# Twenty-four one-pass float32r products ahead of one FFN1 block of a gated-attention and multiplicative-FFN kernel

## The chip, the cores and the metric

The kernel runs on one core of one Trainium2 chip. The core has five engines that run their own instruction streams: PE (TensorE, matrix products), DVE (VectorE), ACT (ScalarE), POOL (GpSimd) and SP (SyncE, which here only starts transfers). They meet at semaphores. The metric is the device time of one execution in microseconds (us); the time of a kernel is the median of its runs.

## The reference, cut to what matters

```python
# attention: 4 batches, 8 heads, 768 positions, head size 48
for t in range(S):
    S_re, S_im = ar * S_re - ai * S_im + kv, ar * S_im + ai * S_re   # kv = outer(k_t, v_t), a clipped to magnitude 0.999
    y[:, :, t] = einsum('bhd,bhde->bhe', q[:, :, t], S_re)
# bridge: x is 3072 tokens x 384
# FFN, d_ff = 1024
a = x @ w1
b = x @ w2
h = a * b @ w3          # (a * b) @ w3
out = h @ w_out
```

Everything is float32. (Some lines are contracted here.)

## The kernel before, in words

The 3072 tokens are cut into eight **units** u = 0 to 7; a unit is half of one batch, 384 positions (TT), and has three chunks of 128. For a unit the kernel does:

- the **gates** (`gates`, elementwise work on tiles of 128x1152 on ACT and DVE): logarithms, exponentials, running products and angles turn the complex recurrence into scaled q and k; 12 transfers of SP then move them to the layout that PE reads (tiles `KL`, `QL`);
- the **attention** on PE: transposes (`turn`, L766, tile `tp`, copied out by ACT at L768), the state (`state`, L830, `kv`), scores inside a chunk (`scores`, L780, `sc`, masked by DVE at L783 into `A`), outputs (`outputs`, L813, `y`), which ACT copies to `xT` (L815), 128 x 3 x 384: the unit's tokens, transposed, with the 384 channels in three rows of 128;
- **FFN1** (`ffn_ab`): for each of eight blocks j of 128 hidden channels two halves. The first half is three products of 128x128 (weights `w1s`) by 128x384 (`xT`) into a PSUM tile `m` (L852), copied by ACT to `a` (L857). The second is the same with `w2s`, and DVE multiplies its PSUM tile with `a` into `ab` (L859);
- **FFN2** with `w3 @ w_out`, multiplied out once at the start (`fuse`, L1150). Two tiles of tokens at a time are done with seven smaller products in place of eight (`out_pair`, L912, tile `p`), on sums that DVE forms (`out_sums`, L887, `So`); DVE and ACT add the products up, SP writes the result out.

PE's program is one list that `pieces`, `ffn` and `unit` put together: the attention of unit u+1 is laid between the FFN of unit u. So FFN1 of unit 3 stands in the list of unit 4: eight halves (blocks 0 to 3) at its head, then the rest between unit 4's transposes and states. The gate work on ACT and DVE is laid beside this list by a planner with an estimated clock per engine (`run`, `fill`, `TIMES`); whatever it decides, each engine then executes its instructions strictly in the order in which they were written down. The planner counts time per list item by `TIMES`, not by the instructions that an item's function issues.

Two rings of buffers matter for the change. PSUM tiles `m` come from `ps_m`, four buffers in turn; a buffer is written again when the one who read it four allocations ago is done. The tiles `a` come from `two` with the tag "a", two buffers in turn.

POOL runs a check over the weights and gates through the whole middle of the program (L1036 to L1072, tiles `look` and `seen`); nobody waits for it until the end.

Of the kernel before, what the change touches and what calls it, by code (L numbers as in the profile page):

```python
# [9 lines left out]

FP = mybir.dt.float32
I32 = mybir.dt.int32
U32 = mybir.dt.uint32
U16 = mybir.dt.uint16
# [10 lines left out]
def general(ctx, tc, qt, kt, v, art, ait, w1, w2, w3t, wo, w1s, w2s, w3o, ident, out):  # L25
# [42 lines left out]

    Qb = [singles.tile([P, 3, S], FP, name=f"Q{i}") for i in range(2)]
    Kb = [singles.tile([P, 2, S], FP, name=f"K{i}") for i in range(2)]  # L70
    Xb = [singles.tile([P, 3, S], FP, name=f"X{i}") for i in range(2)]
    Ab = [singles.tile([P, 2, NC, C], FP, name=f"A{i}") for i in range(2)]
    Db = [singles.tile([P, 2, NC, SB], FP, name=f"D{i}") for i in range(2)]

    sl = singles.tile([P, SB], I32, name="sl")
    nc.gpsimd.iota(sl, pattern=[[0, SB]], base=0, channel_multiplier=1)
    nc.vector.tensor_scalar(out=sl, in0=sl, scalar1=SB - 1, scalar2=None, op0=OP.bitwise_and)
    diag = singles.tile([P, SB], I32, name="diag")  # L80
    nc.gpsimd.iota(diag, pattern=[[1, SB]], base=0, channel_multiplier=0)
    nc.vector.tensor_tensor(out=diag, in0=sl, in1=diag, op=OP.is_equal)
    masks = {}
    for i, n in enumerate((1, 2, 4, 8, 16)):
        m = singles.tile([P, SB // 2], I32, name=f"mask{n}")
        half = singles.tile([P, SB // 2], I32, name=f"half{n}")
        nc.gpsimd.iota(m, pattern=[[2, SB // 2 // n], [0, n]], base=0, channel_multiplier=0)
# [7 lines left out]
    def load_unit(u):  # L95
# [6 lines left out]
        e0 = 2 * hp * D  # L102
        v_t[u] = two.tile([P, NC, 2 * D], FP, tag="v", name="v")
        nc.sync.dma_start(out=v_t[u], in_=v[b, :, e0:e0 + 2 * D].rearrange("(c p) e -> p c e", p=C))
# [197 lines left out]
    def weights(dst, src):  # L302
        if src.dtype == FP:
            return [lambda: nc.sync.dma_start(out=dst, in_=src)]
        r, m = dst.shape[1:]
        src = src.bitcast(I32)
        step = min(r, max(1, LOAD // m)), min(m, LOAD)
# [4 lines left out]
    def convert(dst, src):  # L312
        r, m = dst.shape[1:]
        raw = two.tile([P, r, m, 2], I32, tag="raw", name="raw")
        nc.sync.dma_start(out=raw.rearrange("p r m w -> p r (m w)"), in_=src)
# [61 lines left out]
def kernel(  # L377
# [36 lines left out]
    nc = tc.nc  # L414
    B, H, D, S = qt.shape
    P = 128
# [4 lines left out]
    KD = DM // P  # L421
    DG = P // H
    KF = FF // P
    WB = 2 * P
    HEAD = 16
    VLOAD = 3
    SIGN_DVE = (1,)
    SPLIT = (0,)
    TT = S // 2
# [28 lines left out]
    two = fast.enter_context(tc.tile_pool(name="two", bufs=2))  # L458
    ps_s = fast.enter_context(tc.tile_pool(name="ps_s", bufs=1, space=PSUM))
    ps_v = fast.enter_context(tc.tile_pool(name="ps_v", bufs=2, space=PSUM))  # L460
    ps_m = fast.enter_context(tc.tile_pool(name="ps_m", bufs=4, space=PSUM))
# [33 lines left out]
    g_t, L_t, xT_t, ab_t, T_t, KT_t = {}, {}, {}, {}, {}, {}  # L495
# [49 lines left out]
    def load_v(u):  # L545
        b, h = divmod(u, 2)


        vr = one.tile([P, UC, DM], FP, tag="vr", name="vr")
        nc.sync.dma_start(out=vr, in_=v[b, h * TT:(h + 1) * TT].rearrange("(c p) e -> p c e", p=C))  # L550
        g_t[u]["vr"] = vr
# [292 lines left out]
    def ffn_ab(u, j):  # L844
        got = []

        def half(w):
            if j == 0 and not got:
                ab_t[u] = one.tile([P, KF, TT], FP, tag="ab", name="ab")
            m = ps_m.tile([P, TT], FP, tag="mm", name="m")  # L850
            for f in range(KD):
                nc.tensor.matmul(out=m, lhsT=w[:, j * P // WB, f, j * P % WB:j * P % WB + P], rhs=xT_t[u][:, f],  # L852
                                 start=(f == 0), stop=(f == KD - 1))
            with tc.high_priority():
                if not got:
                    got.append(two.tile([P, TT], FP, tag="a", name="a"))
                    nc.scalar.copy(out=got[0], in_=m)  # L857
                else:
                    last["ab", u, j] = nc.vector.tensor_tensor(out=ab_t[u][:, j], in0=m, in1=got[0], op=OP.mult)  # L859
        return [("ab1", lambda: half(w1s)), ("ab2", lambda: half(w2s))]  # L860
# [7 lines left out]
    def out_weights():  # L868
        T = s_t["T"] = late[0].tile([P, 4, KH, DH], FP, tag="T", name="To")
        B = [[w3o[:, i * KH:(i + 1) * KH, j * DH:(j + 1) * DH] for j in range(2)] for i in range(2)]  # L870
        s_t["B"] = B[0][0], B[1][0], B[1][1], T[:, 3], T[:, 0], T[:, 1], T[:, 2]
        for i, x, y in ((0, B[0][1], B[0][0]), (1, B[1][1], T[:, 0]), (2, B[1][1], B[0][1]), (3, B[1][0], T[:, 1])):
            yield "DVE", 0.96, "out", ()
            nc.vector.tensor_tensor(out=T[:, i], in0=x, in1=y, op=OP.subtract)
# [212 lines left out]
    got = {}  # L1087
# [36 lines left out]
    def row_load(f, parts=1):  # L1124

        step = FF // parts
        w3_t[f] = fetch([columns(w3t, 0, step)[:, f:f + 1], words(wo)[:, f:f + 1]] +
                        [columns(w3t, n * step, (n + 1) * step)[:, f:f + 1] for n in range(1, parts)],
                        {0: "KL", 1: "QL"}.get(f % 4))
# [58 lines left out]
    def pieces(u):  # L1188

        sc = [[("sc", lambda c=c, x=x: scores(u, c, x)) for x in range(2)] for c in range(UC)]  # L1190
        tr = [[("tr", lambda c=c, x=x: turn(u, c, x)) for x in range(2)] for c in range(UC)]
        kv = [("kv0" if u % 2 == c == 0 else "kv" if c < UC - 1 else "rho", lambda c=c: state(u, c)) for c in range(UC)]
        y = [("y" if u % 2 or c else "y0", lambda c=c: outputs(u, c)) for c in range(UC)]

        if u % 2:
            return [[("need", u), tr[0][0]], [tr[0][1]], [tr[1][0], kv[0]], [tr[1][1]], [kv[1]], sc[0], sc[1] + [y[0]],
                    sc[2] + [y[1], y[2], ("end", u)]]
        return [[("need", u), tr[0][0]], [tr[0][1]], [tr[1][0], kv[0]], [tr[1][1]], [tr[2][0], kv[1]], [tr[2][1]],
                [kv[2]] + sc[0], sc[1] + [y[0]], sc[2] + [y[1], y[2], ("end", u)]]
# [19 lines left out]
    def mixed(items, fills, at):  # L1219

        seq = []
        for n, x in enumerate(items + [None]):
            seq += [fills[i] for i, k in enumerate(at) if k == n] + [x]
        return seq[:-1]

    def unit(u, rest, ahead):

        if u == 1:
            return [("begin", u)] + mixed([x for p in pieces(u) for x in p], rest, FILLS[1])
        seq = [("begin", u)] + rest[:ahead]  # L1230
        rest = rest[ahead:]
        p = pieces(u) + [[]]
        n = len(p)
        first = [i * (len(rest) - 2) // (n - 1) for i in range(n)] + [len(rest)]
        for i in range(n):
            seq += rest[first[i]:first[i + 1]] + p[i]
        return seq
# [43 lines left out]
    def run(seq):  # L1281
# [78 lines left out]

        heads = [k for k, (kind, f) in enumerate(seq) if kind == "ab1"][:HEAD // 2:2]
        for o in urgent:
# [50 lines left out]
    with tc.manual_schedule(engines={mybir.EngineType.PE}):  # L1413
# [9 lines left out]
        for f in range(KF):  # L1423
# [3 lines left out]
            if f + 4 < KF:  # L1427
                row_load(f + 4)
            if f == VLOAD:
                load_v(0)  # L1430
# [13 lines left out]
        with tc.manual_schedule(engines={mybir.EngineType.Activation, mybir.EngineType.DVE, mybir.EngineType.Pool, mybir.EngineType.SP}):  # L1444
# [12 lines left out]
            def head(i):  # L1457
                if i % 4 == 0:
                    force(i // 4)
                rest[i][1]()  # L1460
                if i == HEAD - 4:
                    phase.close()
                    late.append(fast.enter_context(tc.tile_pool(name="late", bufs=1)))
                    late.append(fast.enter_context(tc.tile_pool(name="looks", bufs=1)))
                    looks.append(check_weights(late[1]))
                    streams.append((1, out_weights()))
            seq = mixed([x for p in pieces(0) for x in p], fills, FILLS[0]) + [("begin", 0)] + [(rest[i][0], lambda i=i: head(i)) for i in range(HEAD)]
            for u in range(1, NU):
                seq += unit(u, rest[HEAD:] if u == 1 else ffn(u - 1), AHEAD[u])
            seq += ffn(NU - 1)  # L1470
# [43 lines left out]
```

## Time and profile before

| what | value |
|---|---|
| runs | 548.92, 553.14, 553.48 us; median 553.14 |
| span of the profiled execution, first to last instruction | 548.1 us (0.8 us less than the fastest run) |
| PE busy | 518.6 us, 95% of the span |
| DVE, POOL, ACT busy | 374.4, 358.3, 275.2 us |
| share of PE in the chain that ended last | 78% |
| granted TensorE clock, mean | 0.990 |

The profiled execution's own time is not listed apart from its span; the fastest run lies 0.8 us above the span. How to read the rows of the profile: start and duration in us, engine, line, operation, output<-inputs, shape, count; in square brackets the idle time of the engine before it and who ended it. One float32 product of the program is two MATMUL instructions in the trace, each with a weight load (LDWEIGHTS, shown as PEld). The end of a matmul is modelled and lies past the start of the next one, so rates are read from starts, or from the pieces of the chain, not from the mean duration.

### The profile page before, as it was taken

The numbers are of one execution on the slowest core, as the hardware profiler recorded it, in microseconds if no ns is written. First come the engines' busy times: TensorE is split into PE (matmuls) and PEld (weight loads), VectorE is DVE, ScalarE is ACT, GpSimd is POOL, SyncE is SP. The second block draws the span as 40 slices with busy tenths as digits, with TensorE's granted clock in tenths as the row PEclk, the third lists the DMA queues.
The fourth block names the chain that finished last, engine by engine and source line by source line (L and its number), as shares of the span: only waits on it lengthen the run. The fifth ranks groups of instructions, "written<-read, shape, count | busy, mean of one in ns | idle before, by whom it ended". The sixth has DMA issues, their size and how long they took to land.

```text
span 548.1 us, 13443 instructions
## 1 busy us (share of the span) xinstructions
PE 518.6 (95%) x5546; PEld 368.5 (67%) x5546; DVE 374.4 (68%) x553; ACT 275.2 (50%) x391; POOL 358.3 (65%) x425
## 2 busy tenths in 40 slices
PE   5789879999999999989999999999999999999995
PEld 2345565556656885569568875697569866795585
DVE  7999597856585678776877987596859851531162
ACT  6988856655543555665467326834593222111100
POOL 1000000017898888888888889988989988888830
PEclk9899899999999999999999999999999999999999
DMA  9999667485659725593898347925883183123201
GB/s 272 360 407 275 159 227 205 137 185 141 162 135 229 214 96 129 146 215 106 226 241 195 128 131 187 217 85 140 198 198 110 44 210 89 49 72 90 72 25 40
DMA packets 73510, 89.73 MB, mean 164 GB/s; under 512 B 31840, under 2 KB 63264, under 8 KB 72672
## 3 DMA queue, kind: packets, MB, share of 16 engines
q1 hardware_dynamic: 67360, 69.78, 47.7%
q0 software_dynamic: 6080, 19.01, 11.8%
q8 instruction: 45, 0.74, 0.5%
q14 instruction: 25, 0.20, 0.1%
HBM read 65.14 MB, written 4.72 MB: 127 GB/s over the span
## 4 chain that ended last, share of the span: by engine, by line
PE 78%; DVE 9%; ACT 5%; issue 3%; DMA 3%; SPq 1%; DVEq 0%; ACTq 0%
PE m L852 37%; PE p L912 16%; PE y L813 7%; PE sc L780 5%; PE f L1150 3%; PE o L948 3%; PE kv L830 3%; PE tp L766 2%; DMA im<-in_a_im_dram 1%; DVE gZ L687 1%; PE sc L1150 1%; ACT gZ L586 1%; DMA raw<-in_w_dram 1%; ACT re L586 1%; ACT low L1002 1%
## 5 line engine op out<-in xcount | busy, mean ns | idle before, releaser
L852 PE MATMUL m<-xT,w1s 128*128 128x384 f32 x384 | 134.5, 487 | 1.1 <-ACT xT L815 1.1
L852 PE MATMUL m<-xT,w2s 128*128 128x384 f32 x384 | 134.9, 487 | 0.0
L852 PEld LDWEIGHTS m<-xT,w1s 128*128 128x128 f32 x384 | 72.2, 190 | 49.1 <-ACT xT L815 1.7
L852 PEld LDWEIGHTS m<-xT,w2s 128*128 128x128 f32 x384 | 72.0, 190 | 48.0
L1069 POOL TENSOR_SCALAR look<-look 128x256 f32<-128x256 f32 (+1 forms) x84 | 90.2, 1074 | 7.3
L859 DVE TENSOR_TENSOR ab<-m,a 128x384 f32<-128x384 f32 x64 | 35.2, 552 | 82.1 <-PE m L852 74.2
L857 ACT COPY a<-m 128x384 f32<-128x384 f32 x64 | 30.4, 475 | 105.5 <-PE m L852 105.5
L1050 POOL TENSOR_TENSOR seen<-seen,look 128x256 bf16<-128x256 bf16 (+1 forms) x84 | 75.8, 902 | 6.8
L1034 POOL MEMSET seen<- 128x256 bf16 x1 | 0.3, 312 | 115.4 <-DVE ab L859 115.4
L1068 POOL TENSOR_SCALAR look<-look 128x256 f32<-128x256 f32 (+1 forms) x44 | 51.0, 1160 | 7.5 <-DMA look<-in_a_re_dram 4.3
L1066 POOL TENSOR_TENSOR look<-look 128x256 f32<-128x256 f32 (+1 forms) x72 | 52.8, 733 | 1.9
L912 PE MATMUL p<-To,So 128*128 128x192 f32 x240 | 44.1, 332 | 0.0
L1045 POOL DMA_DIRECT2D look<-in_w_dram x56 | 33.2, 592 | 16.6 <-POOL seen L1050 16.6
L815 ACT COPY xT<-y 128x384 f32<-128x384 f32 x24 | 11.5, 480 | 64.2 <-PE y L813 64.2
L813 PE MATMUL y<-A,V 128*32 128x128 f32 x768 | 40.3, 273 | 2.2 <-issue 2.2
L768 ACT COPY KT<-tp 128x384 f32<-128x384 f32 x40 | 34.0, 862 | 14.0 <-PE tp L766 13.6
L912 PEld LDWEIGHTS p<-To,So 128*128 128x128 f32 x240 | 38.7, 190 | 2.2 <-issue 1.8
L1071 POOL TENSOR_TENSOR look<-look 128x256 f32<-128x256 f32 (+1 forms) x44 | 36.2, 824 | 3.7
L813 PEld LDWEIGHTS y<-A,V 128*32 128x32 f32 x768 | 34.7, 110 | 4.2 <-issue 4.2
L1150 PE MATMUL f<-wo_s,w3s 128*128 128x384 f32 x96 | 36.5, 532 | 0.0
L813 PE MATMUL y<-QL,T 96*32 96x128 f32 x640 | 35.7, 272 | 0.6 <-issue 0.6
L783 DVE COPY_PREDICATED A<-mask,sc 128x512 f32<-128x512 uint8 x48 | 32.8, 735 | 3.8 <-PE sc L780 3.6
(129 smaller groups left out, 919.5 us busy)
## 6 DMA issues: line engine op xcount, KB each, us to landing
look<-in_w_dram POOLq DMA_DIRECT2D x56, 256.0 KB, 3.4
raw<-in_w_dram SPq DMA_DIRECT2D x6, 1024.0 KB, 10.1
KL<-gR SPq DMA_DIRECT2D x24, 192.5 KB, 4.3
KL<-k SPq DMA_DIRECT2D x24, 192.5 KB, 5.8
re<-in_a_re_dram SPq DMA_DIRECT2D x24, 192.0 KB, 3.7
im<-in_a_im_dram SPq DMA_DIRECT2D x24, 192.0 KB, 3.5
k<-in_k_dram SPq DMA_DIRECT2D x24, 192.0 KB, 7.5
q<-in_q_dram SPq DMA_DIRECT2D x24, 192.0 KB, 7.3
```

Of the source, the lines that this page charges most:

```text
L768: nc.scalar.copy(out=KT_t[u, c][:, :, :, x].rearrange("p h d f -> p f d h"), in_=tp.rearrange("p f (d h) -> p f d h", h=H))
L813: nc.tensor.matmul(out=o, lhsT=a, rhs=b, start=s0, stop=s1)
L852: nc.tensor.matmul(out=m, lhsT=w[:, j * P // WB, f, j * P % WB:j * P % WB + P], rhs=xT_t[u][:, f], start=(f == 0), stop=(f == KD - 1))
L859: last["ab", u, j] = nc.vector.tensor_tensor(out=ab_t[u][:, j], in0=m, in1=got[0], op=OP.mult)
L912: nc.tensor.matmul(out=m[p], lhsT=a[:, f], rhs=b[:, f], start=(f == 0), stop=(f == KH - 1))
L1045: nc.gpsimd.dma_start(out=got.bitcast(I32)[:, 0:group[2]], in_=group[1])
L1050: nc.gpsimd.tensor_tensor(out=seen[:, 0:n], in0=seen[:, 0:n], in1=x, op=OP.add)
L1066: tt(out=x, in0=x, in1=x, op=OP.mult)
L1068: ts(out=y, in0=x, scalar1=high, scalar2=None, op0=OP.is_le)
L1069: ts(out=x, in0=x, scalar1=low, scalar2=None, op0=OP.is_ge)
L1071: tt(out=x, in0=x, in1=y, op=OP.mult)
L1150: nc.tensor.matmul(out=sums[j], lhsT=w3_t[f][:, j * P:(j + 1) * P], rhs=w3_t["wo"][:, f], start=(f == 0), stop=(f == KF - 1))
```

## The change

One helper of `ffn_ab` gets a few lines, which run once, ahead of the first half of block 4 of unit 3. ACT copies the first row of `xT` (128x384) into a tile `one_pass` of type float32r. PE then multiplies it with itself 24 times: the weights are one of its three 128x128 pieces, the moving operand the whole 128x384, and all 24 accumulate into one PSUM tile. That tile takes one turn of `ps_m`, and `one_pass` one turn of the tag "a". Nobody reads the products.

```diff
+FR = mybir.dt.float32r
...
+    EXTRA = 24
...
             if j == 0 and not got:
                 ab_t[u] = one.tile([P, KF, TT], FP, tag="ab", name="ab")
+            if (u, j) == (3, KF // 2) and not got:
+                one_pass = two.tile([P, TT], FR, tag="a", name="one_pass")
+                nc.scalar.copy(out=one_pass, in_=xT_t[u][:, 0])
+                m = ps_m.tile([P, TT], FP, tag="mm", name="m")
+                for i in range(EXTRA):
+                    nc.tensor.matmul(out=m, lhsT=one_pass[:, i % KD * P:(i % KD + 1) * P], rhs=one_pass, start=(i == 0),
+                                     stop=(i == EXTRA - 1))
             m = ps_m.tile([P, TT], FP, tag="mm", name="m")
             for f in range(KD):
                 nc.tensor.matmul(out=m, lhsT=w[:, j * P // WB, f, j * P % WB:j * P % WB + P], rhs=xT_t[u][:, f],
```

The rest of every engine's list keeps its order. What stands at the place on PE, at the end of block 3 and in block 4 and 5 of unit 3's FFN1 before the change (`m` are the PSUM tiles of the halves, `tp` a transpose of unit 4):

```order
L852 MATMUL m_2706<-xT_2445,w1s_58 128x384 x3
L852 MATMUL m_2719<-xT_2445,w2s_59 128x384 x3
L852 MATMUL m_2729<-xT_2445,w1s_58 128x384 x3
L852 MATMUL m_2769<-xT_2445,w2s_59 128x384 x3
L766 MATMUL tp_2775<-ident_61,gR_2201 128x128 x3
L852 MATMUL m_2780<-xT_2445,w1s_58 128x384 x3
```

And on PE at the same place with the change (later lines have moved by nine line numbers):

```order
L861 MATMUL m_2706<-xT_2445,w1s_58 128x384 x3
L861 MATMUL m_2719<-xT_2445,w2s_59 128x384 x3
L857 MATMUL m_2731<-one_pass_2729 128x384 x24
L861 MATMUL m_2756<-xT_2445,w1s_58 128x384 x3
L861 MATMUL m_2796<-xT_2445,w2s_59 128x384 x3
L768 MATMUL tp_2802<-ident_61,gR_2201 128x128 x3
L861 MATMUL m_2807<-xT_2445,w1s_58 128x384 x3
```

The 24 products stand between the second half of block 3 and the first half of block 4, and nothing else has moved. On ACT, the same stretch before, from the copy of block 3's first half (`re` and `gZ` are gate work of unit 4, `KT` the copies of its transposes):

```order
L586 ACTIVATE re_2106<-re_2106,consts_100 128x1152
L857 COPY a_2710<-m_2706 128x384
L586 ACTIVATE gZ_2202<-gZ_2202 128x1152
L857 COPY a_2733<-m_2729 128x384
L592 ACT_TABLE_LOAD
L586 ACTIVATE gA_2759<-re_2661 128x1152
```

And on ACT with the change:

```order
L588 ACTIVATE re_2106<-re_2106,consts_100 128x1152
L866 COPY a_2710<-m_2706 128x384
L588 ACTIVATE gZ_2202<-gZ_2202 128x1152
L854 CAST one_pass_2729<-xT_2445 128x384
L866 COPY a_2760<-m_2756 128x384
L594 ACT_TABLE_LOAD
L588 ACTIVATE gA_2786<-re_2661 128x1152
```

The new copy stands behind one piece of gate work (`gZ`) and ahead of the copy of block 4's first half. DVE, POOL and SP have the same rows in the same order as before.

## The prediction

> **What bounds the kernel now.** I read the page's head first: which engine is busy, and whether evenly.
>
> ```profile
> span 548.1 us, 13443 instructions
> PE 518.6 (95%) x5546; PEld 368.5 (67%) x5546; DVE 374.4 (68%) x553; ACT 275.2 (50%) x391; POOL 358.3 (65%) x425
> ...
> PE   5789879999999999989999999999999999999995
> ...
> PEclk9899899999999999999999999999999999999999
> ```
>
> PE is at 95%, and the slices say that its idle time lies almost all in the first eighth; from slice 7 on nearly every digit is a 9, at full granted clock. A busy share alone can mislead, since a matmul's end is modelled. So the next view is the chain of work that ended last, in order of time, from the place of the change (FFN1 of unit 3 runs from 258.81) to the end:
>
> ```profile
> 258.81 19.35 PE m L852 x60
> 278.16 0.33 PE tp L766 x3
> 278.49 3.87 PE m L852 x12
> ...
> 300.26 2.62 PE p L912 x16
> 302.87 0.02 issue
> 302.90 0.36 DVE ot L894
> 303.25 0.61 DVE So L887
> ...
> 306.00 1.10 DVE So L887
> 307.09 0.47 DVE T L836
> 307.57 0.02 issue
> 307.59 0.55 DVE T L839
> 308.14 0.65 DVE A L783
> 308.79 0.04 issue
> 308.84 1.39 PE sc L780 x64
> ...
> 492.68 30.96 PE m L852 x96
> 523.64 6.50 PE p L912 x40
> 530.26 11.91 PE p L912 x72
> ```
>
> The chain is PE without a break from 258.81 to 302.87. It then runs over DVE for 5.9 us and comes back to PE, and it ends on PE. Even the stretch over DVE hangs on PE: it begins when the products at 300.26 are done. The third view is the list of waits from 258 us to the end; PE has one entry in it that waits for another engine:
>
> ```profile
> PE sc L780 <- DVE A L783: 1.5, 2, 1.0
> ```
>
> So in the 290 us behind the place of the change PE waits 1.5 us in all. Whatever holds PE up there reaches the end, unless it shortens one of these two waits.
>
> **What the change adds.** One ACT instruction and 24 products, nothing removed, no row moved against another on any engine. Four costs have to be worked out: the products, the wait for their operand, what is queued behind, and the buffers.
>
> *The products.* A float32 product of 128x128x384 is two MATMUL instructions in the trace. The chain's first piece has 60 of them in 19.35 us, 0.3225 us each, 0.645 us per product. The FFN2 products have half as many columns, and 16 instructions take 2.62 us: 0.164 us each. Halving the columns halves the time, so these streams are bound by columns passed, with nothing fixed worth naming. Now how many passes is one instruction? The transposes (one instruction per 128x128 block) are the only rows that come once per operation of the program: three take 0.33 us, 0.11 us for 128 columns, where 0.3225 us for 384 columns would make 0.1075. That alone decides nothing, since a transpose may be bound by its weight load. Here no row decides, so the bounds: a product cannot be shorter than the 128-column transpose (0.11 us; 24 make 2.6 us), nor longer than the float32 product (0.645 us; 15.5 us). If float32 is four passes, two per instruction, then one pass of 384 columns is as long as an FFN2 instruction, two passes of 192: 0.164 us. I take this, 24 x 0.164 = 3.9 us. The FFN2 row also shows that a fresh 128x128 weight load every 0.164 us is sustained, which is the rate needed here.
>
> The Trainium skill, in "FP8 and Floating Point Precision", section "TensorE Precision Notes", states that true FP32 takes four passes through the array, and that there is a reduced-precision form which truncates to FP22. By it a product costs a quarter of 0.645 us, 0.161 us, and 24 cost 3.9 us, as in the sum above; no run here shows float32r yet.
>
> *The wait for the operand.* The copy to `one_pass` stands on ACT behind `gZ`, and PE cannot begin before it. ACT and PE at the place:
>
> ```profile
> 272.28 1.26 ACT L586 ACTIVATE re<-re,consts 128x1152 f32<-128x1152 f32 x1
> ...
> 273.45 0.46 ACT L857 COPY a<-m 128x384 f32<-128x384 f32 x1
> 273.81 1.16 ACT L586 ACTIVATE gZ<-gZ 128x1152 f32<-128x1152 f32 x1
> 276.26 0.48 ACT L857 COPY a<-m 128x384 f32<-128x384 f32 x1 [1.29 <-PE m L852]
> 276.76 1.28 ACT L592 ACT_TABLE_LOAD   x1
> 278.05 1.16 ACT L586 ACTIVATE gA<-re 128x1152 f32<-128x1152 f32 x1
> 279.12 0.85 ACT L768 COPY KT<-tp 128x384 f32<-128x384 f32 x1
> ```
>
> ```profile
> 272.19 2.10 PE L852 MATMUL m<-xT,w2s 128*128 128x384 f32 x6
> 274.12 2.10 PE L852 MATMUL m<-xT,w1s 128*128 128x384 f32 x6
> ```
>
> PE would start block 4 at 274.12, and that is where the first product wants its operand. But ACT starts `gZ` only at 273.81. An instruction behind a 1.16 us one starts 1.07 us later (278.05 to 279.12), so the copy starts at 274.88. Its length, between two copies from SBUF:
>
> ```profile
> L878 ACT COPY kept<-ab 128x1024 f32<-128x1024 f32 x3 | 3.1, 1048 | 0.0
> ...
> L661 ACT COPY k<-gA 128x3 f32<-128x3 f32 x7 | 1.4, 195 | 0.0
> ```
>
> From 3 to 1024 columns it grows by 853 ns, 0.84 ns a column, so 384 columns take 0.195 + 0.32 = 0.51 us, near the 0.46 to 0.48 us of the copies `a` above; I take 0.49. The output type is new, and a tenth up or down is the bound. The copy ends at 275.37. Hand-over from ACT to PE, from the state products that waited for a copy:
>
> ```profile
> 236.53 1.52 ACT L768 COPY KT<-tp 128x384 f32<-128x384 f32 x2
> ...
> 238.10 0.88 PE L830 MATMUL kv<-vr,KT 128*32 128x48 f32 x48
> ```
>
> 236.53 + 1.52 = 238.05, and PE starts at 238.10: 0.05 us. So the products start at 275.42, a new PE wait of 275.42 - 274.12 = **1.3 us**. Nothing covers it: PE executes in order, and what it could do meanwhile stands behind the products. Bounds: 0 if ACT had been ahead by one instruction, 2.5 us if it were behind by another piece of gate work of 1.16 us.
>
> *Behind it.* On ACT the copy of block 4's first half, a table load and the gate work of unit 5 wait for PE as before, and come 5.2 us later. That harms nobody: they wait for PE already now (the 1.29 us of idle at 276.26), and their consumers on PE come 5.2 us later too. DVE had been late at this place, and catches up, but it waits for PE again a block later, so it brings no lead to 303:
>
> ```profile
> 279.79 0.54 DVE L859 TENSOR_TENSOR ab<-m,a 128x384 f32<-128x384 f32 x1
> 282.47 0.56 DVE L859 TENSOR_TENSOR ab<-m,a 128x384 f32<-128x384 f32 x1 [2.13 <-PE tp L766]
> ```
>
> So I count no recovery of the wait at 308.84; all of the 1.5 us is the bound. SP's transfers for unit 4 hang on DVE's products and start at the same time as before, which is earlier for PE.
>
> *The buffers.* The extra `m` takes one turn of four, the extra `a` one of two; the copy overwrites what DVE read for block 2, in a row that starts at 270.98, done before 274.88. The next blocks ask for buffers one turn younger, but all are free by 275.4 (block 3's `ab` starts at 274.85 and takes 0.55), while block 4 now starts at 279.4. Cost nothing; if the products did not push block 4 back, this cover would be gone and block 4 would wait some tenths.
>
> ```profile
> 270.98 0.54 DVE L859 TENSOR_TENSOR ab<-m,a 128x384 f32<-128x384 f32 x1
> ...
> 274.85 0.55 DVE L859 TENSOR_TENSOR ab<-m,a 128x384 f32<-128x384 f32 x1
> ```
>
> **The sum**: 3.9 + 1.3 = 5.2 us, a span of 553.3 after 548.1. Against times: the profiled execution's span is 0.8 us under the fastest run and 5.0 under the median of 553.14; two of three runs lie near the median. The addition is one of work and not of a share, so I put it on the median: **558.3 us**, +0.95%. One per cent, 5.5 us, is about what a measurement of this kernel can tell from no change; the forecast lies just within it.
>
> **The rivals.**
>
> *Weight loads not hidden (slower).* In the two-instruction products of float32, the next load may hide because each product brings two instructions; in a one-pass stream each load could stand between the products. Its price is at most a whole transpose, which has a load and a third of the columns: 0.164 + 0.11 = 0.274 us, 6.6 us for 24, 7.9 us with the wait, **561.0 us** (+1.4%). It decides from 0.013 us of unhidden load per product, where the sum passes 5.5 us. Against it stands the FFN2 row, a load per 0.164 us instruction with no gap.
>
> The Trainium skill, "TensorE: Matmul & The Clock Gate", Part 3 ("Packing small matmuls — row/col tiling"), says that a weight load overlaps a running matmul only when the two use different row groups; all 128 rows are used here, so by it this rival is the case. The trace disagrees, with 16 loads and 16 matmuls on 128 rows in 2.62 us. Chance 0.09.
>
> *float32r is no cheaper than float32 (the change does not do what it says).* Then 24 x 0.645 = 15.5 us and 1.3: 16.8, **569.9 us**; with one instruction of two passes, 24 x 0.3225 + 1.3 = 9.0, 562.1. For it: no row of this trace has the type. Chance 0.08.
>
> *Cheaper.* ACT is ahead in most executions and the wait goes, or the wait at 308.84 shrinks, or products approach the transpose's 0.11 us: between 3.9 - 1.5 = 2.4 us and 4.2 us, **555.5 to 557.3**. For it: ACT idles 1.29 us right behind `gZ`, so it is not loaded there. Against: its order is fixed, and it is busy from 272.28 to 274.97. Chance 0.09.
>
> *Nothing to see.* The products, which nobody reads, cost no time in the end: 553.1. Only an idle PE could do that, and it has 1.5 us. Chance 0.04.
>
> **How the numbers follow.** The forecast has the rest, 0.70. Its own spread is 0.4 us of the terms, and a median that can fall on the lower or the higher of runs 4 us apart: 554 to 559.5. To hold 8 in 10, the range goes up past the unhidden loads, to 561.5, and down to 553.0 for the cheaper case and a low median; full-price products and most of "nothing" stay out. Faster by over 1%: 0.03, from low medians alone. Slower by over 1%: 0.28 of the forecast's 0.70, since 0.95% is that near the bound, 0.08 from the loads and 0.08 from full price, 0.45 with rounding. Within: 0.52.
>
> **What will show it.** A group of L857 on PE with 24 matmuls, 0.164 us from start to start, in a piece of 3.9 us: the products. 0.27 us says unhidden loads, 0.32 or 0.645 more passes. A PE wait of 1.3 us for ACT `one_pass`, ahead of them: the second term. Every later PE row, the first `sc` of unit 4 at 308.84 included, 5.2 us later with its 1.0 us wait kept: no recovery. The prediction is wrong above all if float32r has a rate of its own, or if the chain behind the place is less rigid than one execution shows.

## The result, and the profile after

| | before | changed |
|---|---|---|
| median of 18 runs each, us | 549.36 (546.69 to 555.40) | 556.08 (552.53 to 561.11) |
| ratio | | 1.0108, 95% interval 1.0078 to 1.0137 |
| span of the profiled execution, us | 548.1 | 556.4 |

The change costs 5.9 us by the ratio (4.3 to 7.5), 6.7 us between the medians. The 18 runs of the kernel before have a median 3.8 us under that of the three shown ahead of the prediction. The profiled execution of the changed kernel took 558.26 us, 2.2 us more than the median, so it is not the typical one.

The page's head and slices of the changed kernel:

```profile
span 556.4 us, 13492 instructions
PE 525.1 (94%) x5570; PEld 374.5 (67%) x5570; DVE 372.9 (67%) x553; ACT 274.8 (49%) x392; POOL 357.6 (64%) x425
...
PEclk9889799999999999999999999999999999999999
```

24 more matmuls, 24 more weight loads, one more ACT instruction. PE's busy time grew by 6.5 us, the span by 8.3. The chain of work that ended last, around the place:

```profile
270.34 1.76 DVE gZ L704
...
272.12 1.17 ACT re L588
...
273.31 1.25 ACT re L588
274.57 0.36 ACT a L866
274.93 1.06 ACT gZ L588
276.00 0.41 ACT one_pass L854
276.41 0.04 issue
276.45 6.02 PE m L857 x24
282.47 3.87 PE m L861 x12
```

Before, this stretch of the chain was PE alone. Now it comes in over gate work on DVE and ACT and the new copy. PE's rows in order of time:

```profile
272.46 2.10 PE L861 MATMUL m<-xT,w2s 128*128 128x384 f32 x6
276.45 6.02 PE L857 MATMUL m<-one_pass 128*128 128x384 f32 x24 [1.89 <-ACT one_pass L854]
282.31 2.10 PE L861 MATMUL m<-xT,w1s 128*128 128x384 f32 x6
```

Six instructions of 0.3225 us from 272.46 end at 274.39, where PE would have gone on; it does at 276.45, a wait of 2.06 us (the row's 1.89 counts from a modelled end). The products take until 282.31, 5.86 us, 0.244 each. The sum for these two executions: block 4 starts at 282.31 where it started at 274.12, 8.19 us later: 0.27 that PE was late already, 2.06 and 5.86. That leaves 0.1 us of the 8.3 for the 274 us behind it, which is a net figure: PE gained there and lost again, as shown further down. At the place itself neither term is as predicted. The clock, in three adjoining stretches; the columns are the stretch, its length, the busy time of PE, PEld, DVE, ACT and POOL with their instructions, the granted clock, and DMA's share and GB/s:

```profile
273.90:277.31 3.41, 1.52 (x8) 0.90 (x7) 2.71 (x3) 2.50 (x4) 3.00 (x4) 1.00 0.78 218
277.31:280.72 3.41, 3.41 (x13) 3.41 (x11) 3.41 (x3) 0.00 (x0) 3.00 (x4) 0.50 0.56 171
280.72:284.13 3.41, 3.41 (x16) 2.73 (x16) 0.22 (x1) 0.00 (x0) 3.08 (x5) 1.00 1.00 271
```

From 277.31 to 280.72 PE ran at half clock. From start to start, the products are mostly 0.174 us apart ahead of that stretch, 0.173 to 0.185 behind it, and 0.320 us inside. The slices of the page round this away (9 of 10 there).

### The profile page after: what moved, and what is told of

Same layout as the page of the kernel before. It is cut to its first block, busy times and chain, and to the rows that moved or that the text cites. A ratio compares the mean times of both kernels' runs of the same rounds, so it can differ in the third digit from the quotient of the medians.

```text
span 556.4 us, 13492 instructions
## 1 busy us (share of the span) xinstructions
PE 525.1 (94%) x5570; PEld 374.5 (67%) x5570; DVE 372.9 (67%) x553; ACT 274.8 (49%) x392; POOL 357.6 (64%) x425
## 4 chain that ended last, share of the span: by engine, by line
PE 77%; DVE 11%; ACT 4%; DMA 3%; issue 3%; SPq 1%; DVEq 0%; ACTq 0%
PE m L861 38%; PE p L921 15%; PE y L815 6%; PE sc L782 5%; PE f L1159 3%; PE o L957 3%; PE kv L832 2%; PE tp L768 2%; DMA im<-in_a_im_dram 2%; DVE So L896 1%; PE sc L1159 1%; ACT gZ L588 1%; DVE gZ L689 1%; PE m L857 1%; DMA raw<-in_w_dram 1%
## 5 line engine op out<-in xcount | busy, mean ns | idle before, releaser
L1078 POOL TENSOR_SCALAR look<-look 128x256 f32<-128x256 f32 (+1 forms) x84 | 86.0, 1024 | 7.3
L1059 POOL TENSOR_TENSOR seen<-seen,look 128x256 bf16<-128x256 bf16 (+1 forms) x84 | 77.2, 919 | 6.8
L1077 POOL TENSOR_SCALAR look<-look 128x256 f32<-128x256 f32 (+1 forms) x44 | 50.2, 1140 | 7.6 <-DMA look<-in_a_re_dram 4.3
L1075 POOL TENSOR_TENSOR look<-look 128x256 f32<-128x256 f32 (+1 forms) x72 | 52.9, 735 | 1.9
L1080 POOL TENSOR_TENSOR look<-look 128x256 f32<-128x256 f32 (+1 forms) x44 | 39.2, 892 | 3.7
```

What stands on the lines that cost most here:

```text
L1059: nc.gpsimd.tensor_tensor(out=seen[:, 0:n], in0=seen[:, 0:n], in1=x, op=OP.add)
L1075: tt(out=x, in0=x, in1=x, op=OP.mult)
L1077: ts(out=y, in0=x, scalar1=high, scalar2=None, op0=OP.is_le)
L1078: ts(out=x, in0=x, scalar1=low, scalar2=None, op0=OP.is_ge)
L1080: tt(out=x, in0=x, in1=y, op=OP.mult)
```

## The experiments

Two readings of the 0.244 us. **A**: the wait ahead of the products made the clock drop, and the products themselves take 0.174. **B**: a float32r stream is slow by itself, by weight loads that do not hide or a rate of its own. "Over the kernel before" in microseconds is the ratio's interval times 549.

**e1: the copy one place earlier on ACT**, right behind block 3's copy and so ahead of `gZ`; PE's list is the changed kernel's.

```diff
             if (u, j) == (3, KF // 2) and not got:
-                one_pass = two.tile([P, TT], FR, tag="a", name="one_pass")
-                nc.scalar.copy(out=one_pass, in_=xT_t[u][:, 0])
+                one_pass = g_t["one_pass"]
...
                     nc.scalar.copy(out=got[0], in_=m)
+                    if (u, j) == (3, KF // 2 - 1):
+                        g_t["one_pass"] = two.tile([P, TT], FR, tag="a", name="one_pass")
+                        nc.scalar.copy(out=g_t["one_pass"], in_=xT_t[u][:, 0])
```

> The copy to one_pass is written one place earlier on ACT, ahead of the gate work gZ and right behind the copy of block 3; PE's list and the buffers are as in the changed kernel. Theory A (the wait lowers the clock): PE waits 0 to 0.7 us in place of 2.06, no stretch at half clock, 24 products in 4.2 us (0.174 each); +4.2 to +4.9 us over the kernel before. Theory B (a float32r stream is slow by itself, weight loads in the open or a rate of its own): the products take 5.9 us again whatever the wait, half of them 0.32 us apart; +5.9 to +6.6 us.

Ratio 1.0104 (1.0069 to 1.0140): +3.8 to +7.7 us. On ACT and PE:

```profile
274.19 0.51 ACT L868 CAST one_pass<-xT 128x384 fp32r<-128x384 f32 x1
274.60 1.17 ACT L588 ACTIVATE gZ<-gZ 128x1152 f32<-128x1152 f32 x1
```

```profile
272.62 2.10 PE L860 MATMUL m<-xT,w2s 128*128 128x384 f32 x6
274.75 4.44 PE L856 MATMUL m<-one_pass 128*128 128x384 f32 x24
279.03 2.10 PE L860 MATMUL m<-xT,w1s 128*128 128x384 f32 x6
```

The wait is 0.2 us (274.75 against 272.62 + 1.935), the products take 4.28 us, the clock stays full. Theory B is out. By this trace the kernel should cost 4.5 us, which is in the lower part of the interval. The run times do not tell this kernel from the changed one (+5.7 against +5.9 us by the ratio); only the traces, of one execution each, do.

**e2: the products half a block later on PE**, the copy where the change put it.

```diff
             if (u, j) == (3, KF // 2) and not got:
-                one_pass = two.tile([P, TT], FR, tag="a", name="one_pass")
+                one_pass = g_t["one_pass"] = two.tile([P, TT], FR, tag="a", name="one_pass")
                 nc.scalar.copy(out=one_pass, in_=xT_t[u][:, 0])
+            if (u, j) == (3, KF // 2) and got:
+                one_pass = g_t["one_pass"]
                 m = ps_m.tile([P, TT], FP, tag="mm", name="m")
                 for i in range(EXTRA):
```

> The copy stays where it is on ACT; the 24 products stand half a block later on PE, behind the first half of block 4, so that the copy has 1.9 us more. Theory A: no wait at all, no stretch at half clock, 24 products in 4.2 us; +4.2 us over the kernel before. Theory B: 5.9 us for the products; +5.9 us.

Ratio 1.0105 (1.0066 to 1.0144), +3.6 to +7.9 us; median 553.44 against 548.76 in the same session, +4.7. From the chain:

```profile
256.97 17.41 PE m L863 x54
274.39 4.16 PE m L859 x24
278.55 1.94 PE m L863 x6
```

No wait, no half clock, 24 products in 4.16 us: 0.173 each. As theory A has it; its +4.2 lies inside the interval, in the lower part.

**e3 and e4: one product, and 48**, with `EXTRA` set to 1 and to 48.

> One float32r product in place of 24, at the place of the change; the copy and PE's wait for it are kept. Theory A: a wait of 1.3 to 2.1 us, 0.17 us for the product, and in about half of the runs 3.4 us at half clock that now fall on float32 products of FFN1 (0.64 us from start to start in place of 0.32) and cost 1.7 us: +1.5 to +4.0 us, the median near +2.8. Theory B: the wait and the product alone, clock full: +1.5 to +2.3 us.

> 48 products in place of 24 at the place of the change. Theory A: the further 24 run at full clock, 0.174 us each: +4.2 us over the changed kernel (+10.1 to +10.9 over the kernel before), and a half-clock stretch, where there is one, is still 3.4 us long. Theory B: the further 24 cost what the first did, +5.9 us over the changed kernel, and 24 of 48 starts are 0.32 us apart.

e3: ratio 1.0015 (0.9989 to 1.0041), -0.6 to +2.3 us. e4: 1.0177 (1.0132 to 1.0223), +7.2 to +12.2. PE's rows of e3, then of e4:

```profile
269.32 2.10 PE L861 MATMUL m<-xT,w2s 128*128 128x384 f32 x6
272.50 0.44 PE L857 MATMUL m<-one_pass 128*128 128x384 f32 x1 [1.08 <-ACT one_pass L854]
272.79 2.10 PE L861 MATMUL m<-xT,w1s 128*128 128x384 f32 x6
```

```profile
271.66 2.10 PE L861 MATMUL m<-xT,w2s 128*128 128x384 f32 x6
274.98 8.59 PE L857 MATMUL m<-one_pass 128*128 128x384 f32 x48 [1.23 <-ACT one_pass L854]
283.41 0.81 PE L861 MATMUL m<-xT,w1s 128*128 128x384 f32 x2
```

Waits of 1.25 and 1.39 us, and no half clock behind either. One product takes 0.29 us to the next row, 48 take 8.43: the 47 that follow the first cost 0.173 each. So the price per product is settled, and "a wait ahead of the stream drops the clock" is too simple: these waits did not. The times agree: theory A's median of +2.8 us for e3 lies outside the interval, while wait and product alone (1.25 + 0.29 = 1.5 us) lie inside. The granted clock changes on a raster of 3.41 us, and what differed is how long PE was idle inside one stretch of it. In e4 PE was busy for 2.40 us of the stretch that held most of the wait, in e3 for 2.86 and 2.89 of the two that shared it, in the changed kernel for 1.52. I call this A2: the clock halves for a stretch if PE was busy for less than about two fifths of the stretch before it.

**e7: the changed kernel again; e5 and e6: the same with 4 and 10 more copies** of `xT` rows into `one_pass` ahead of the one that counts, to lengthen the wait. One execution each.

```diff
-                nc.scalar.copy(out=one_pass, in_=xT_t[u][:, 0])
+                for f in (1, 2, 1, 2, 0):            # e6: (1, 2) * 5 + (0,)
+                    nc.scalar.copy(out=one_pass, in_=xT_t[u][:, f])
```

> The changed kernel again, one more look. Theory A2 (the clock halves for the next 3.41 us where PE was busy for less than about two fifths of a 3.41 us stretch): PE waits 1.2 to 2.1 us at the products; a half-clock stretch only if the wait is near 2 us or over and falls into one stretch, else 24 products in 4.3 us. Theory B (any wait ahead of the stream lowers the clock): a half-clock stretch again.

> Four more copies of 128x384 into one_pass ahead of the one that counts, 0.36 us each: PE waits 2.7 to 3.5 us in place of 1.2 to 2.1. Theory A2: a half-clock stretch behind it with a chance of about two in three, since 2.05 us of the wait must lie in one stretch; products 5.4 to 5.9 us then, else 4.3 us. If waits had nothing to do with the clock: 4.3 us and no stretch.

> Ten more copies ahead: PE waits 4.8 to 5.7 us. Theory A2: a half-clock stretch for certain, which begins inside the wait or at its end; the part of its 3.41 us that lies behind the wait slows the products (0.32 us a start), which then take between 4.3 and 6.0 us. If waits had nothing to do with the clock: no stretch and 4.3 us.

In e7 PE waits again, 1.85 us (275.66 against 271.88 + 1.935), but at full clock; 24 products take 4.27 us:

```profile
271.88 2.10 PE L861 MATMUL m<-xT,w2s 128*128 128x384 f32 x6
275.66 4.43 PE L857 MATMUL m<-one_pass 128*128 128x384 f32 x24 [1.68 <-ACT one_pass L854]
279.93 2.10 PE L861 MATMUL m<-xT,w1s 128*128 128x384 f32 x6
```

The raster fell so that its wait was cut in two (a stretch ends at 275.09). The clock of this execution dropped elsewhere, at 237.54, behind an old wait for `KT` that the kernel before has too; so a half-clock stretch needs no float32r product. The stretches of e7 at both places; the first two rows show PE alone (length, PE busy, clock, DMA), the last two all engines as above:

```profile
234.12:237.54 3.42, 1.03 (x19) 1.00 1.11 238
237.54:240.95 3.41, 3.41 (x55) 0.50 1.08 239
...
271.68:275.09 3.41, 2.30 (x8) 1.02 (x6) 1.36 (x3) 3.38 (x4) 2.91 (x5) 1.00 0.83 233
275.09:278.51 3.42, 2.85 (x16) 2.85 (x17) 3.42 (x5) 0.52 (x2) 3.25 (x3) 1.00 0.45 131
```

e5, then e6, the same view of PE alone:

```profile
274.51:277.93 3.42, 1.23 (x7) 1.00 0.62 174
277.93:281.34 3.41, 3.41 (x13) 0.50 0.98 276
```

```profile
275.32:278.73 3.41, 0.00 (x0) 1.00 0.82 253
278.73:285.56 6.83, 4.35 (x14) 0.50 1.00 243
```

e5 waits 3.4 us and gets the half-clock stretch, e6 waits 6.6 us and gets two of them; products 5.84 and 6.27 us, the latter over the 6.0 expected, since the second stretch was not foreseen. e6's copies came 0.54 us apart, not 0.36, so its wait is longer than expected. The times of these single executions are 555.46 (e7), 558.21 (e5) and 562.59 us (e6), with 552.01 for one of the kernel before.

Behind 100 us, over all eleven traces of this document, stretches with at most 1.52 us of PE busy were followed by half clock and those with 1.54 or more were not. In the changed kernel's first profile a stretch of 3.5 us that does not follow the raster, 235.30 to 238.80, has PE busy for only 1.12 us and no half clock behind it; on the raster PE was busy for 2.52 and 1.93 us there. So the raster counts.

The limit itself does not hold ahead of 100 us. First e2, then the changed kernel, each with the stretch that follows:

```profile
34.61:38.02 3.41, 1.44 (x5) 1.00 1.02 418
38.02:41.44 3.42, 3.10 (x10) 1.00 0.99 392
```

```profile
58.86:62.27 3.41, 1.79 (x54) 1.00 0.94 244
62.27:65.68 3.41, 2.68 (x39) 0.50 0.48 75
```

In e2, 1.44 us of float32 products with 384 columns were enough to keep the clock; in the changed kernel 1.79 us of transposes (`tp`) and narrow state products (`kv`) were not. So A2 fits in kind, as far as these traces go: what PE did in the stretch before decides. But the busy time of this view alone is not its measure, and what else counts stays open.

**e8: fewer columns.** At e2's place, four groups of 24 products with 384, 256, 192 and 128 columns, each with its own weight load.

```diff
-                for i in range(EXTRA):
-                    nc.tensor.matmul(out=m, ..., rhs=one_pass, ...)
+                for n in (384, 256, 192, 128):
+                    for i in range(EXTRA):
+                        nc.tensor.matmul(out=m[:, 0:n], ..., rhs=one_pass[:, 0:n], ...)
```

> At the place without a wait, four groups of 24 float32r products with 384, 256, 192 and 128 columns moved, all with a weight load of 128x128 for each. If columns set the pace (0.42 ns each) with 0.0135 us fixed per product: 0.174, 0.120, 0.094 and 0.067 us from start to start. If hidden weight loads set it from below, at the 0.11 us of a transpose: 0.174, 0.12, 0.11, 0.11. If loads lie in the open: 0.174 minus 0.053 for each 128 columns less, so 0.067 at 128 would exclude it.

The groups by shape; the means include a modelled tail, so only their steps are read:

```profile
L860 PE MATMUL m<-one_pass 128*128 128x384 f32 x24 | 4.6, 348 | 0.0
L860 PE MATMUL m<-one_pass 128*128 128x256 f32 x24 | 3.0, 283 | 0.0
L860 PE MATMUL m<-one_pass 128*128 128x192 f32 x24 | 2.8, 274 | 0.0
L860 PE MATMUL m<-one_pass 128*128 128x128 f32 x24 | 2.8, 274 | 0.0
```

Typical distances from start to start are 0.173, 0.120, 0.111 and 0.111 us. That is the second case expected. From 384 to 256 columns the price falls by 0.053, about 0.42 ns a column; at 192 it meets a floor of 0.111 and stays there. Loads in the open would add to the columns and show no floor, so they are out. That the floor is the wait for the next hidden weight load fits, since a transpose with its own load has the same distance (0.109), but no run takes the load away, so it is not shown.

**e9: float32 in place of float32r**, at e2's place.

```diff
-                one_pass = g_t["one_pass"] = two.tile([P, TT], FR, tag="a", name="one_pass")
+                one_pass = g_t["one_pass"] = two.tile([P, TT], FP, tag="a", name="one_pass")
```

> The 24 products in float32 in place of float32r (the copy keeps float32), at the place without a wait. If one float32r product is one pass and one float32 product four: two instructions of 0.3225 us per product, 15.5 us for 24 where the float32r ones took 4.2 us; +15.5 us over the kernel before (ratio 1.028). If float32r were not what makes the products short: 4.2 us again.

Ratio 1.0246 (1.0210 to 1.0281): +11.5 to +15.4 us; median 563.34 against 548.54, +14.8. In the chain:

```profile
274.53 15.48 PE m L859 x48
```

48 instructions, 0.3225 us each, as predicted from FFN1's rows. 15.48 against 4.16 in e2: a float32r product costs 0.27 of a float32 one, a little over a quarter. The interval of the times ends just under the +15.5 expected, and its middle is 2 us lower; the runs do not show why. The profiled execution took 563.63 us, the slowest of the four.

## Why the prediction was right or wrong

**The frame held.** Slower, and just about one per cent: +5.9 us (4.3 to 7.5) against +5.2. The measured 556.08 us lies in the range, 2.2 us under the forecast of 558.3. How near it came is partly luck: the forecast was put on a median of three runs (553.14) that 18 runs show as 549.36, 3.8 us too high, and the cost between the medians is 6.7 us, 1.5 more than the sum. In the 18 runs of the changed kernel the time is 1.8 to 2.0 us more than the span. By this, as an estimate, the span of 548.1 stood for an execution of about 550.0 us, near the true median, and would have been the better base. The executions of one kernel differ by more than the change costs (546.69 to 555.40 us before). Some of that arises ahead of the place: block 4 of unit 3 (or the products ahead of it) was due between 270.8 us (e8) and 274.7 us (e6).

**No recovery: right in the net, wrong in the step.** From block 4's start to the end of the span there are 274.0 us before (548.1 - 274.12) and 274.1 after (556.4 - 282.31); in e1, e3, e4 and e7, 272.8 to 274.9. So what PE loses here reaches the end, to within about 1 us. But the prediction's own sign, the `sc` row at 308.84, which was to keep its wait of 1.0 us, did not. This row and two rows of DVE ahead of it, before and after:

```profile
303.89 1.10 DVE L887 TENSOR_TENSOR So<-So,kept 128x512 f32<-128x512 f32 x1
304.91 1.16 DVE L887 TENSOR_TENSOR So<-kept,ab 128x512 f32<-128x512 f32 x1
...
308.84 1.39 PE L780 MATMUL sc<-QL,KL 96*32 96x128 f32 x64 [1.03 <-DVE A L783]
```

```profile
312.07 0.82 DVE L896 TENSOR_TENSOR So<-So,kept 128x512 f32<-128x512 f32 x1
312.81 0.68 DVE L896 TENSOR_TENSOR So<-kept,ab 128x512 f32<-128x512 f32 x1
...
316.25 1.40 PE L782 MATMUL sc<-QL,KL 96*32 96x128 f32 x64 [0.26 <-DVE A L785]
```

The rows of DVE took 0.76 us less, and PE's wait shrank from 1.03 to 0.26 us: `sc` comes 7.41 us later where block 4 came 8.19 later. Another 0.27 us is won by 318.9. Later waits give most of it back, above all one for DVE at 433.35, which is 1.07 us long in place of 0.51, and PE's last row comes 7.9 us later. That the net is nothing is luck of these two executions; the gain lies inside the 1.5 us that the prediction gave as its bound. The step that failed is that the length of DVE's work behind the place would stay the same. The wait is 0.30 to 0.45 us in e3, e4, e5, e6 and e7 too, where PE waited for `one_pass`, and 1.11 and 0.97 in e1 and e2, where it waited for 0.2 us and not at all. Why DVE's rows differ is not shown.

**The products: the size was off.** 24 x 0.164 = 3.9 us was the sum; at full clock they take 4.16 us (e2), or 4.27 with a first one of 0.28 behind a wait. The step that failed is the rate taken from the FFN2 instruction: the column part is as read (0.42 ns), but a float32r product carries 0.012 us beside it (0.173 - 384 x 0.00042), which a float32 instruction does not (0.3225 - 768 x 0.00042 = 0). The runs do not show what it is; in the half-clock stretch nothing is left of it (0.320 is no more than twice 0.161). The reading of one pass against four fits e9.

**The wait: right in kind, low in size.** 1.3 us was computed from one execution, and e3 and e4 show 1.25 and 1.39; the changed kernel itself showed 2.06 and 1.85. The step that failed is to treat the time of `gZ` against PE as fixed. It ends a chain of gate work over DVE and ACT (in the changed kernel's chain back to 259.47) that does not run in step with PE. e1 shows the term by itself: one row earlier on ACT and the wait falls to 0.2 us. The other parts of the term hold: the copy took 0.50 us, the hand-over 0.04 us (276.41 to 276.45).

**The half clock: missing from the sum.** In the profiled execution it costs 5.86 - 4.27 = 1.6 us; e7, the same kernel, had none at this place. So it is a price that some executions pay, and the runs do not say how many. The mean granted clock of the 18 runs is 0.987, and that of the 18 of the kernel before in e1's session 0.985, while one more stretch of 3.41 us at half clock takes 0.003 off; so these means show no general loss at half clock. The prediction saw waits, and no cost beyond their length: it took the full granted clock of the trace before as given. The Trainium skill, "TensorE: Matmul & The Clock Gate", Part 1, says that the clock halves after at least one idle window of about 3.4 us, on windows that run free of the kernel, which by itself would have excluded a drop after 2 us. The trace agrees on the window (3.41 us), on the half and on its free run, and differs on idleness: 1.52 us of work in the window did not prevent it, nor 1.03 in e7.

**The rivals.** "Weight loads not hidden" gave 7.9 us at the place, and the profiled execution shows just that sum (2.06 + 5.86 = 7.9), by another mechanism: a warning that a sum can fit for a wrong reason. The 0.173 us per product of e2, and e8, where the distance stays at 0.111 from 192 to 128 columns, exclude it. So the rule of the Trainium skill, "TensorE: Matmul & The Clock Gate", Part 3, by which loads overlap only across row groups, does not hold for these streams: the measurement decides. "No cheaper than float32" is out by e9. "Cheaper", with ACT ahead of PE, is the case in neither of the two profiled executions of the changed kernel. "Nothing to see" is out by the interval of the times (4.3 to 7.5 us).

## What to carry to other kernels

An instruction that feeds PE from another engine costs where it stands in that engine's queue: move the copy one row ahead of a 1.2 us piece of work, or its consumer half a block later, and the wait falls to 0.2 us or to nothing, while the products cost the same. The traces show this; the saving is too small to stand out in the run times here. On a PE that is seldom idle, read a new wait's place as well as its length, since 2 us of idle time in one clock stretch cost another 1.6 us here. A wait further on that one trace shows is no constant either: it shrank when the rows ahead of it got shorter. Compare rates from start to start and look at the granted clock in stretches of a few microseconds before a slow stream is blamed on the instruction.

## What the runs showed of the hardware that was not expected

- A one-pass float32r product with its own 128x128 weights has a floor of 0.111 us from start to start, for 192 and for 128 columns; above it 0.42 ns per column and 0.012 us.
- The half-clock stretch came after a stretch with PE busy for 1.52 us of 3.41 (45% by the modelled ends), behind 100 us never with 1.54 or more. Ahead of 100 us, 1.44 us of 384-column products kept the clock and 1.79 us of transposes and state products lost it.
- One more such stretch comes right behind the kernel's old wait for `KT` near 235 us in e3 and e7 (2.29 and 2.23 us), but not in the profiled execution before, whose raster cut a wait of 1.58 us in two.
